# Local attention in units of 58 queries and 64 keys, both heads of a pair in one transpose

## The chip, the cores and the metric

One core of a Trainium2 chip runs the whole program. The metric is the device time of one execution in microseconds (us). PE (TensorE) does matrix products and transposes, DVE (VectorE), ACT (ScalarE) and POOL (GpSimd) work on elements, SP only issues DMAs.

## What is computed

Three stages in a row; the change touches the first alone. Here S = 576, D = 64, four sequences of eight heads.

```python
q_d, k_d, v_d = means over groups of 4 positions          # 144 groups
out_d = softmax(q_d @ k_d.T / 8) @ v_d                     # the "down" half
mask = abs(pos[:, None] - pos[None, :]) < 4                # 7 keys a query
out_local = softmax(where(mask, q @ k.T / 8, -1e9)) @ v    # the "local" half
x = repeat(out_d, 4) + out_local                           # 2304 tokens x 512
x = (silu(x @ w_gate) * (x @ w_val)) @ w_out               # 512 -> 1536 -> 512
# then each token goes to one of 8 experts: relu(x @ w1[e]) @ w2[e], times its gate
```

## The kernel before, in words

Heads are taken two at a time: 16 **pairs**, n = 0 to 15, four to a sequence b. A pair has five slots of 128 x 1024 floats: `sq` (queries, later also sums), `sk` (keys), `sv` (values for the local half), `sd` (values for the down half), `sa` (local scores). In `sq` and `sk` the first head has partitions 0 to 63, the second 64 to 127.

**Local half** (`local`, L569; `local_piece`, L610). Nine units of 64 queries with a window of 70 keys. L582 makes the scores of a unit, two units stacked to a block of 128 partitions x 70; L588 adds the mask, L591 to L601 take the softmax over 700 columns with L595 on ACT, and L603 on POOL divides. L628 transposes each block of each head by itself (70 x 128), in three pieces; ACT copies them out of PSUM at L632 and L636, the two large ones into `sd`, which first has to be free of the down half (`vfree`). L652 multiplies with the values, 70 rows deep, both heads of a pair into the two halves of one PSUM bank; L659 on DVE adds the down half and writes `x32`.

**Down half** (`down`, L491). L496 sums groups of four, L506 makes scores, L522 exponentials, L531 divides, L539 transposes, and L556 multiplies with v. For pairs 0 to 7 (`n < NE`) the sum of four values is left to L556 as sixteen products (profiles and traces count an fp32 product as two instructions, so 32 there); for pairs 8 to 15 POOL sums first (`down_v`, L486 and L488) and L556 has four products.

**Gated layer.** 9 chunks of 256 tokens; L750 is the first product (gate and val), L782 the second. The first two chunks go through the six weight blocks together, as the blocks come. A weight block is decoded from 64-bit words: L339 (DVE), L342 and L346 (ACT), L349 (DVE), L354 (ACT), L356 (POOL). Sequence 0 supplies chunk 0 and 1, sequence 1 is worked off beside these chunks' products, sequences 2 and 3 beside chunks 2 to 5. For pairs 4 to 7 the two heads' scores are made one after the other (`head_sets`).

**Order.** The program writes its instructions with a planner (`Sched`): every step is a task with a priority and a cost in ns, and the planner's simulated time decides the order in which the steps stand on each engine. At run time each engine takes its list strictly in that order. So any change of a cost or a dependency can move steps everywhere. While nothing is ready before the first chunk, `keep_warm` fills PE with products that nobody reads (L314). Pairs 4 to 7 reuse the slots of pairs 0 to 3, and their loads stand on SP among the weight loads (L330).

Of the kernel before, what the change touches and what calls it, by code (L numbers as in the profile page):

```python
# [19 lines left out]
ALU = mybir.AluOpType  # L20
# [12 lines left out]
NU = S // 64  # L33
WK = 70
NPAIR = (NU + 1) // 2
# [30 lines left out]
def t_act(n): return 170 + 0.85 * n  # L66
# [140 lines left out]
EARLY_N = range(NE)  # L207
WEIGHT_P = [1.0, 2.0, 3.0, 4.0, 4.5, 4.8]


def build(tc, a):
# [26 lines left out]
    def dma(n):  # L238
        return ("op", "DMA", t_dma(n), None)
# [197 lines left out]
    def heads(n):  # L437
        b, hp = divmod(n, HP)
        cls, tk = ("we", "early") if n in EARLY_N else ("aw", "late")
        if b > 1:  # L440

            for j in range(2):
                yield ("wait", ("w_out", NFB - 1, j))
        yield ("get", tk)
        sl = []
        for _ in range(5):
            sl.append((yield ("get", cls)))
        sq, sk, sv, sd, sa = sl
        src = a["qk"][b, hp]
        yield dma(P * 1158 * 4)  # L450
# [40 lines left out]
    def down(n, sq, sk, sd):  # L491

        qd = sq[:, S:S + 2 * G].rearrange("p (j g) -> p j g", j=2)
# [4 lines left out]
        st = sk[:GH, 710:726].rearrange("p (i x) -> p i x", i=4)  # L498
# [59 lines left out]
        if n < NE:  # L558
            sc.set(("vfree", n))
        yield op("ACT", t_act(G))  # L560
        nc.scalar.copy(sq[:, S + 2 * G:S + 3 * G], av[:, 0:G])
# [5 lines left out]
    def local(n, sq, sk, sv, sa, st):  # L567
# [3 lines left out]
        A = sa[:, 0:2 * m].rearrange("p (h c) -> p h c", h=2)  # L571
        A3 = sa[:, 0:2 * m].rearrange("p (x w) -> p x w", w=WK)
        mx, s1 = sa[:, 2 * m:2 * m + 2 * NPAIR], sa[:, 2 * m + 2 * NPAIR:2 * m + 4 * NPAIR]
        bc = lambda x: x.unsqueeze(2).to_broadcast([P, 2 * NPAIR, WK])
        for hs in head_sets(n):
            sp = yield from pget(len(hs))
            yield op("PE", 1000)
            for u in range(2 * NPAIR):
                uu = min(u, NU - 1)
                for h2, s in zip(hs, sp):  # L580
                    r = slice(h2 * D, (h2 + 1) * D)
                    nc.tensor.matmul(s[(u % 2) * 64:(u % 2) * 64 + 64, u // 2 * WK:(u // 2 + 1) * WK],  # L582
                                     sq[r, 64 * uu:64 * uu + 64], sk[r, 64 * uu:64 * uu + WK], start=True, stop=True)
            if hs[-1] == 1:
                sc.set(("qk", n))
            for h2, s in zip(hs, sp):
                yield op("DVE", t_dve(m) + 60)
                nc.vector.tensor_tensor(out=A[:, h2], in0=s[:, 0:m], in1=amask, op=ALU.add)  # L588
                pput(s)
# [14 lines left out]
        for jj in range(3):  # L604
            sc.spawn(sc.cur.prio, local_piece(n, jj, sq, sk, sv, sa, st, A))
# [3 lines left out]

    def local_piece(n, jj, sq, sk, sv, sa, st, A):  # L610

        b, hp = divmod(n, HP)
        vl = lambda u: sv[:WK, u * P:(u + 1) * P] if u < NU - 1 else sk[:WK, S + 6:S + 6 + P]
        js = [j for j in (2 * jj, 2 * jj + 1) if j < NPAIR]
        if jj < 2:
# [7 lines left out]
        yield op("PE", 2 * len(js) * 75)  # L623
# [5 lines left out]
        k = 2 * len(js) * P  # L629
        if jj == 2:  # L630
            yield op("ACT", t_act(P))
            nc.scalar.copy(t.rearrange("p (h q) -> p h q", h=2)[:, :, 0:64],  # L632
                           tp[:WK, 0:2 * P].rearrange("p (h q) -> p h q", h=2)[:, :, 0:64])
        else:
            yield op("ACT", t_act(k))
            nc.scalar.copy(t[:, 0:k], tp[:WK, 0:k])  # L636
        pput(tp)
        t0, t1 = 256 * jj, min(S, 256 * jj + 256)
# [5 lines left out]
        yield op("PE", 4 * len(js) * 65)  # L644
        for i, j in enumerate(js):
            for u in (2 * j, 2 * j + 1):
                if u >= NU:
                    continue
                for h2 in range(2):
                    o = (2 * i + h2) * P + u % 2 * 64  # L650
                    c = (u - 4 * jj) * 64
                    nc.tensor.matmul(xp[h2 * D:(h2 + 1) * D, c:c + 64], vl(u)[:, h2 * D:(h2 + 1) * D], t[:, o:o + 64],  # L652
                                     start=True, stop=True)
        up = sq[:, S + 2 * G:S + 3 * G]
        while t0 < t1:
# [5 lines left out]
                in0=xp[:, t0 - 256 * jj:e - 256 * jj].rearrange("p (g f) -> p g f", f=4),  # L661
# [666 lines left out]
def consts():  # L1328

    m = np.full((2, 64, NPAIR, WK), NEG, np.float32)  # L1330
    for u in range(2 * NPAIR):
        for q in range(64):
            for w in range(7):
                key = 64 * min(u, NU - 1) + q + w - 3
                if 0 <= key < S:
                    m[u % 2, q, u // 2, q + w] = 0.0
# [14 lines left out]
def layout(inputs):  # L1351
# [3 lines left out]
    qk = np.zeros((B, HP, 2, D, 2 * S + 6), q.dtype)  # L1355
    qk[..., 0:S] = q.transpose(0, 1, 2, 4, 3)
    qk[..., S + 3:2 * S + 3] = k.transpose(0, 1, 2, 4, 3)
    arr["qk"] = qk.reshape(B, HP, P, 2 * S + 6)

    vp = np.zeros((B, HP, S + 6, 2, D), v.dtype)  # L1360
    vp[:, :, 3:S + 3] = v.transpose(0, 1, 3, 2, 4)
    vv = np.zeros((B, HP, GH, NU * P + 1024), v.dtype)
    for u in range(NU):
        vv[:, :, 0:WK, u * P:(u + 1) * P] = vp[:, :, 64 * u:64 * u + WK].reshape(B, HP, WK, P)
    vv[..., NU * P:] = v.reshape(B, HP, 2, 2, GH, 4 * D).transpose(0, 1, 4, 2, 3, 5).reshape(B, HP, GH, 1024)
    arr["vv"] = vv
# [20 lines left out]
```

## Time and profile before

| | |
|---|---|
| median of 3 runs | 928.62 us (926.08 to 933.64) |
| the profiled execution, its own time | 932.92 us |
| its span, first to last instruction | 931.1 us |
| PE busy | 903.5 us (97%) |
| DVE, ACT, POOL busy | 438.5, 403.1, 279.5 us |

The profile's own time lies 4.3 us above the median of the runs. In its rows a line such as "L628 PE MATMUL" is line 628 of the kernel; two instructions of PE may overlap, so how long a group keeps PE is read from its start to the start of what follows.

### The profile page before, as it was taken

How to read it: one execution, taken by the hardware profiler on the slowest of the kernel's cores; microseconds unless marked ns; L12 is line 12 of the kernel's file. 1: busy time of each engine (PE TensorE's matmuls, PEld its weight loads, DVE VectorE, ACT ScalarE, POOL GpSimd, SP SyncE). 2: the span in 40 equal slices, each digit the busy share in tenths (PEclk: the TensorE clock that was granted, in tenths of full speed). 3: DMA queues.
4: the chain of work that ended last, by engine and by line, in shares of the span. 5: the costliest groups of instructions: out<-in, count | busy, mean ns of one | idle time of the engine just before them, and what ended most of it. 6: DMA issues, size and time to landing. Idle time of an engine off the chain costs nothing. (4 is left out here: it accounts for less than half of the span.)

```text
span 931.1 us, 17520 instructions
## 1 busy us (share of the span) xinstructions
PE 903.5 (97%) x7039; PEld 797.3 (86%) x7046; DVE 438.5 (47%) x1020; ACT 403.1 (43%) x867; POOL 279.5 (30%) x286
## 2 busy tenths in 40 slices
PE   8999899999999999999999999999999999999995
PEld 4688788998999989889999999989888888888883
DVE  4949756744435435454323231456544554544310
ACT  1678679954235224333332231345334444444221
POOL 1335535633324323324212121231220412321211
PEclk9969999999999999999999999999999999999997
DMA  8745334411211212022000000146256544554100
GB/s 211 211 156 167 104 125 136 128 58 50 76 38 40 54 53 70 8 53 76 2 22 3 1 25 1 49 155 204 58 172 201 182 153 162 174 179 134 35 25 27
DMA packets 52869, 87.90 MB, mean 94 GB/s; under 512 B 7982, under 2 KB 25614, under 8 KB 52784
## 3 DMA queue, kind: packets, MB, share of 16 engines
q1 hardware_dynamic: 48048, 76.59, 27.1%
q0 software_dynamic: 4160, 9.48, 3.0%
q8 instruction: 56, 0.92, 0.4%
q10 hardware_dynamic: 576, 0.67, 0.3%
q14 instruction: 29, 0.24, 0.1%
HBM read 77.73 MB, written 10.57 MB: 95 GB/s over the span
## 5 line engine op out<-in xcount | busy, mean ns | idle before, releaser
L750 PE MATMUL ps<-xhi,w 128*128 128x256 f32 x1536 | 304.7, 288 | 2.9 <-ACT aw L522 1.4
L750 PEld LDWEIGHTS ps<-xhi,w 128*128 128x128 f32 x1536 | 247.9, 191 | 10.2 <-issue 3.5
L750 PE MATMUL ps<-xlo,w 128*128 128x256 f32 x768 | 217.6, 283 | 0.3 <-POOL xlo L707 0.3
L750 PEld LDWEIGHTS ps<-xlo,w 128*128 128x128 f32 x768 | 147.3, 192 | 2.0 <-POOL xlo L707 0.5
L720 DVE SCALAR_TENSOR_TENSOR th<-th,ps 128x256 f32<-128x256 f32 x108 | 45.3, 419 | 183.6 <-ACT th L718 183.5
L1076 PE MATMUL ps<-xh,w 128*128 128x336 f32 (+1 forms) x512 | 121.9, 313 | 0.0
L782 PE MATMUL x<-w,hh 128*128 128x512 f32 x384 | 121.2, 397 | 0.4 <-ACT hh L725 0.4
L728 POOL TENSOR_TENSOR hl<-th,hh 128x256 fp32r<-128x256 f32 x90 | 69.7, 774 | 166.3 <-ACT hh L725 136.1
L718 ACT ACTIVATE th<-ps 128x256 f32<-128x256 f32 x108 | 41.7, 386 | 157.9 <-PE ps L750 152.1
L1076 PEld LDWEIGHTS ps<-xh,w 128*128 128x128 f32 x512 | 87.9, 188 | 2.1
L975 DVE TENSOR_TENSOR w<-w,w 128x1024 fp32r<-128x1024 f32 x64 | 77.5, 1224 | 16.2 <-ACT w L973 14.7
L1086 PE MATMUL x<-w,eh 128*128 128x512 f32 x256 | 81.0, 397 | 0.0
L1076 PE MATMUL ps<-xl,w 128*128 128x336 f32 (+1 forms) x256 | 79.8, 312 | 0.0
L782 PEld LDWEIGHTS x<-w,hh 128*128 128x128 f32 x384 | 68.2, 188 | 13.0 <-ACT hh L725 0.8
L1062 DVE SCALAR_TENSOR_TENSOR el<-ps,eh 128x336 fp32r<-128x336 f32 (+1 forms) x64 | 31.5, 492 | 101.0 <-ACT eh L1060 97.8
L1101 POOL DMA_INDIRECT out<-t,tb x23 | 22.9, 994 | 180.1 <-ACT t L1093 165.0
L1060 ACT ACTIVATE eh<-ps 128x336 fp32r<-128x336 f32 (+1 forms) x64 | 28.4, 443 | 108.7 <-PE ps L1076 107.5
L782 PE MATMUL x<-w,hl 128*128 128x512 f32 x192 | 75.0, 390 | 0.2 <-DVE hl L728 0.2
L725 ACT CAST hh<-th 128x256 fp32r<-128x256 f32 x108 | 44.2, 409 | 61.0 <-DVE th L722 60.8
L973 ACT CAST w<-w 128x1024 fp32r<-128x1024 f32 x64 | 66.0, 1044 | 0.0
L1086 PEld LDWEIGHTS x<-w,eh 128*128 128x128 f32 x256 | 46.5, 188 | 9.2
L356 POOL TENSOR_TENSOR w<-w,w 128x512 fp32r<-128x512 f32 x30 | 40.4, 1352 | 36.0 <-ACT w L354 17.4
(195 smaller groups left out, 1464.5 us busy)
## 6 DMA issues: line engine op xcount, KB each, us to landing
w<-w SPq DMA_DIRECT2D x64, 512.0 KB
w<-w_gate SPq DMA_DIRECT2D x10, 512.0 KB
w<-w_val SPq DMA_DIRECT2D x10, 512.0 KB
w<-w_out SPq DMA_DIRECT2D x10, 512.0 KB
x2d<-t SPq DMA_DIRECT2D x18, 256.0 KB
w<-qk SPq DMA_DIRECT2D x8, 291.0 KB
aw<-qk SPq DMA_DIRECT2D x8, 291.0 KB
w<-qk SPq DMA_DIRECT2D x8, 288.0 KB
```

What stands on the lines that cost most here:

```text
L356: nc.gpsimd.tensor_tensor(out=los, in0=lw.bitcast(F32), in1=his, op=ALU.subtract)
L718: nc.scalar.activation(th, ps[:, 0:CT], AF.Tanh, scale=0.5)
L720: nc.vector.scalar_tensor_tensor(out=th, in0=th, scalar=1.0, in1=ps[:, 0:CT], op0=ALU.add, op1=ALU.mult)
L725: nc.scalar.copy(hh[:, j].bitcast(F32R), th)
L728: e.tensor_tensor(out=hl[:, j].bitcast(F32R), in0=th, in1=hh[:, j].bitcast(F32R), op=ALU.subtract)
L750: nc.tensor.matmul(ps[:, o:o + CT], ww[:, k, fs], xx[:, k, :], start=(k == 0 and n == 0), stop=(k == KD - 1 and n == 2))
L782: nc.tensor.matmul(x2p[c, m], l[:, j, ms], r[:, js], start=(p == 0 and j == 0 and n == 0), stop=(p == NFB - 1 and j == 1 and n == 2))
L973: nc.scalar.copy(hi.bitcast(F32R), raw)
L975: nc.vector.tensor_tensor(out=lo.bitcast(F32R), in0=raw, in1=hi.bitcast(F32R), op=ALU.subtract)
L1062: nc.vector.scalar_tensor_tensor(out=hl[:, j, 0:n].bitcast(F32R), in0=ps[:, 0:n], scalar=0.0, in1=hh[:, j, 0:n].bitcast(F32R), op0=ALU.max ...
L1076: nc.tensor.matmul(ps[:, 0:n], ww[:, k, fs], xx[:, k, 0:n], start=(k == 0 and t == 0), stop=(k == KD - 1 and t == 2))
L1086: nc.tensor.matmul(yt[:m], l, r, start=(first and n == 0), stop=(last and n == 2))
```

## The change

Ten units of 58 queries and 64 keys replace nine of 64 and 70. A block of 128 partitions now holds 64 columns of one head and 64 of the other, so one full 128 x 128 transpose does both heads; after it the first head's keys stand on partitions 0 to 63 and the second's on 64 to 127. The values come in that layout as a new input `vw`. The transposed pieces go into free parts of `sv` and `sa` and no longer wait for `vfree`. The sums of v go to POOL for pairs 4 to 7 as well (`NV = 4` in place of `NE = 8`). The pieces end at 232, 464 and 576 queries (256, 512 and 576 before). The scores compute 64 query rows per unit of which 58 are used.

```diff
-NU = S // 64
-WK = 70
-NPAIR = (NU + 1) // 2
+UQ = 58
+NU = -(-S // UQ)
+WK = UQ + 6
+NPAIR = NU // 2
+SP6 = S + 6
+unit0 = lambda u: min(UQ * u, S - UQ)
...
+NV = 4
@@ heads @@
-        nc.sync.dma_start(out=sq[:, 0:S], in_=src[:, 0:S])
-        nc.sync.dma_start(out=sk[:, 0:S + 6], in_=src[:, S:2 * S + 6])
+        nc.sync.dma_start(out=sq[:, 0:SP6], in_=src[:, 0:SP6])
+        nc.sync.dma_start(out=sk[:, 0:SP6], in_=src[:, SP6:2 * SP6])
         sc.cur.t -= sc.LAT_DMA
-        vs = a["vv"][b, hp]
-        yield dma(GH * 2176 * 4)
-        nc.sync.dma_start(out=sv[:WK, :], in_=vs[:WK, 0:1024])
-        nc.sync.dma_start(out=sk[:WK, S + 6:S + 6 + P], in_=vs[:WK, 1024:1152])
-        nc.sync.dma_start(out=sd[:GH, :], in_=vs[:, 1152:2176])
+        yield dma(P * NU * D * 4 + GH * 4096)
+        nc.sync.dma_start(out=sv[:, 0:NU * D], in_=a["vw"][b, hp])
+        nc.sync.dma_start(out=sd[:GH, :], in_=a["vv"][b, hp])
         pr = sc.cur.prio
-        if n >= NE:
+        if n >= NV:
             sc.spawn(pr, down_v(n, sk, sd))
@@ down (the same in both places where n < NE stood) @@
-        if n < NE:
+        if n < NV:
             parts = [sd[:GH, 256 * x + D * i:256 * x + D * (i + 1)] for x in range(4) for i in range(4)]
@@ local @@
-        A = sa[:, 0:2 * m].rearrange("p (h c) -> p h c", h=2)
+        A = sa[:, 0:2 * m].rearrange("p (j h w) -> p j h w", h=2, w=WK)
...
-            for u in range(2 * NPAIR):
-                uu = min(u, NU - 1)
+            for u in range(NU):
+                t0 = unit0(u)
                 for h2, s in zip(hs, sp):
                     r = slice(h2 * D, (h2 + 1) * D)
                     nc.tensor.matmul(s[(u % 2) * 64:(u % 2) * 64 + 64, u // 2 * WK:(u // 2 + 1) * WK],
-                                     sq[r, 64 * uu:64 * uu + 64], sk[r, 64 * uu:64 * uu + WK], start=True, stop=True)
+                                     sq[r, t0:t0 + 64], sk[r, t0:t0 + WK], start=True, stop=True)
...
@@ local_piece @@
-            t = st[:WK, jj * 512:(jj + 1) * 512]
-            yield ("wait", ("vfree", n))
-        else:
-            t = sa[:WK, 740:996]
+        k = len(js) * P
+        t = (sv[:, 640:896], sa[:, 680:936], sv[:, 896:1024])[jj]
         [tp] = yield from pget()
...
         for i, j in enumerate(js):
-            w = min(P, S - j * P)
-            for h2 in range(2):
-                o = (2 * i + h2) * P
-                nc.tensor.transpose(tp[:WK, o:o + w], A[:w, h2, j * WK:(j + 1) * WK], ident[:w, :w])
...
+            nc.tensor.transpose(tp[:, i * P:(i + 1) * P], sa[:, j * P:(j + 1) * P], ident)
+        yield op("ACT", t_act(k))
+        nc.scalar.copy(t, tp[:, 0:k])
         pput(tp)
-        t0, t1 = 256 * jj, min(S, 256 * jj + 256)
+        t0, t1 = 4 * UQ * jj, min(S, 4 * UQ * (jj + 1))
+        p0 = t0
...
-                    nc.tensor.matmul(xp[h2 * D:(h2 + 1) * D, c:c + 64], vl(u)[:, h2 * D:(h2 + 1) * D], t[:, o:o + 64],
-                                     start=True, stop=True)
+                    r = slice(h2 * D, (h2 + 1) * D)
+                    nc.tensor.matmul(xp[r, UQ * u - p0:UQ * u - p0 + UQ - o], sv[r, u * D:(u + 1) * D],
+                                     t[r, i * P + v * 64 + o:i * P + v * 64 + UQ], start=True, stop=True)
```

On PE, in the products of chunk 3, pair 9 of sequence 2 is transposed and multiplied with its values (`ps` is a PSUM bank, `aw` a slot of the pair, `cn` holds the identity; xN counts like rows in a row). Transposes before, and now:

```order
1465 L750 MATMUL ps_1_104<-xhi,w_4_1861 128x256
1466 L628 MATMUL ps_1_103<-cn,aw_3_2730 70x128 x4
1467 L628 MATMUL ps_1_102<-cn,aw_3_2730 70x128 x4
1468 L628 MATMUL ps_1_107<-cn,aw_3_2730 70x64 x2
1469 L750 MATMUL ps_1_106<-xhi,w_5_1698 128x256
```

```order
1471 L740 MATMUL ps_1_102<-xhi,w_3_1774 128x256
1472 L624 MATMUL ps_1_107<-cn,aw_3_2662 128x128 x2
1473 L624 MATMUL ps_1_106<-cn,aw_3_2662 128x128 x2
1474 L624 MATMUL ps_1_103<-cn,aw_3_2662 128x128
1475 L740 MATMUL ps_1_102<-xhi,w_3_1772 128x256
```

Products with v of the same pair, before, and now:

```order
1507 L782 MATMUL x_1_108<-w_3_1687,hl_1_97 128x512
1508 L652 MATMUL ps_1_104<-aw_3_2729,aw_4_2728 64x64 x8
1509 L652 MATMUL ps_1_107<-aw_3_2729,aw_4_2728 64x64 x8
1510 L652 MATMUL ps_1_105<-aw_3_2730,aw_4_2727 64x64 x2
1511 L750 MATMUL ps_1_103<-xhi,w_3_1938 128x256
```

```order
1519 L740 MATMUL ps_1_107<-xhi,w_5_1854 128x256
1520 L642 MATMUL ps_1_103<-aw_4_2660 64x58 x8
1521 L642 MATMUL ps_1_102<-aw_3_2662,aw_4_2660 64x58 x8
1522 L642 MATMUL ps_1_105<-aw_4_2660 64x58 x2
1523 L642 MATMUL ps_1_105<-aw_4_2660 64x54 x2
1524 L740 MATMUL ps_1_107<-xhi,w_6_1853 128x256
```

Ten transposes become five; eighteen products become twenty, and both heads of a piece still go into one bank. The places among the large products are nearly the same.

On SP, where the loads of pairs 5 and 6 meet the second weight block (gate, gate, val, val), before, and now:

```order
34 L451 DMA w_2_645<-qk 128x576
35 L452 DMA w_2_646<-qk 128x582
36 L456 DMA w_2_647<-vv 70x1024
37 L457 DMA w_2_646<-vv 70x128
38 L458 DMA w_2_648<-vv 72x1024
39 L330 DMA w_1_643<-w_gate 128x2x512
40 L330 DMA w_2_702<-w_gate 128x2x512
41 L330 DMA w_2_717<-w_val 128x2x512
42 L451 DMA w_2_797<-qk 128x576
43 L452 DMA w_2_798<-qk 128x582
```

```order
28 L460 DMA w_2_532<-vv 72x1024
29 L334 DMA w_2_505<-w_gate 128x2x512
30 L334 DMA w_2_599<-w_val 128x2x512
31 L455 DMA w_2_650<-qk 128x582
32 L456 DMA w_2_651<-qk 128x582
33 L459 DMA w_2_652<-vw 128x640
34 L460 DMA w_2_653<-vv 72x1024
35 L334 DMA w_2_619<-w_val 128x2x512
36 L455 DMA w_2_766<-qk 128x582
37 L456 DMA w_2_767<-qk 128x582
```

Before, the block's second val load stood behind the loads of pairs 6 and 7; now it stands ahead of both.

On POOL, from the decode of the first weight block on, before, and now (`hl`, `xlo` belong to the gated layer, 72x4x128 and 72x256 are the sums of v):

```order
23 L356 TENSOR_TENSOR w_1_146<-w_1_141,w_1_145 128x512
24 L356 TENSOR_TENSOR w_1_146<-w_1_142,w_1_145 128x512
25 L356 TENSOR_TENSOR w_1_369<-w_1_346,w_1_368 128x512
26 L393 TENSOR_TENSOR ess<-ess,half 8x1
27 L356 TENSOR_TENSOR w_1_369<-w_1_367,w_1_368 128x512
```

```order
19 L360 TENSOR_TENSOR w_1_146<-w_1_141,w_1_145 128x512
20 L360 TENSOR_TENSOR w_1_146<-w_1_142,w_1_145 128x512
21 L697 TENSOR_TENSOR xlo<-x_1_112,xhi 128x256
22 L697 TENSOR_TENSOR aw_1_117<-x_1_113,aw_1_116 128x256
23 L488 TENSOR_TENSOR w_2_532<-w_2_532 72x4x128
24 L360 TENSOR_TENSOR w_1_369<-w_1_346,w_1_368 128x512
25 L490 TENSOR_TENSOR w_2_530<-w_2_532 72x256
26 L606 TENSOR_TENSOR w_1_137<-w_1_137 128x640
```

The sums of pair 4 (w_2_530, w_2_532) now stand ahead of the division of pair 3 (w_1_137), which before stood ahead of the whole decode.

## Rows read from the trace of the kernel before

**Rows 1.** Page: span; busy time, share of the span and instructions of PE and its loads.

```profile
span 931.1 us, 17520 instructions
PE 903.5 (97%) x7039; PEld 797.3 (86%) x7046; DVE 438.5 (47%) x1020; ACT 403.1 (43%) x867; POOL 279.5 (30%) x286
```

**Rows 2.** Stretches: length, busy (instructions) by engine, granted clock, DMA share, GB/s.

```profile
51.10:68.20 17.10, 17.10 (x129) 14.96 (x129) 5.53 (x10) 11.07 (x18) 5.90 (x6) 0.50 0.51 165
68.20:112.60 44.40, 41.20 (x437) 35.56 (x437) 38.79 (x81) 34.58 (x76) 26.13 (x23) 1.00 0.41 120
112.60:119.40 6.80, 6.80 (x32) 5.80 (x30) 1.52 (x6) 2.27 (x8) 2.53 (x3) 0.50 0.68 269
119.40:205.00 85.60, 84.68 (x745) 76.04 (x744) 53.71 (x105) 70.62 (x122) 44.89 (x39) 1.00 0.37 118
205.00:480.00 275.00, 272.67 (x2495) 247.85 (x2494) 123.28 (x385) 96.88 (x281) 87.42 (x100) 1.00 0.16 44
```

**Rows 3.** Groups by line: busy us, mean ns of one, idle before and its releasers.

```profile
L314 PE MATMUL x<-w 128*128 128x512 bf16 x113 | 29.0, 404 | 2.9 <-POOL w L311 2.1 <-issue 0.6 <-DMA w<-vv 0.2
```

**Rows 4.** Order of time on PE, sequences 2 and 3: start us, us, instruction.

```profile
287.12 0.66 PE L827 MATMUL x<-cn,t 128*128 128x128 f32 x4
287.53 0.36 PE L750 MATMUL ps<-xhi,w 128*128 128x256 f32 x1
...
300.19 0.71 PE L556 MATMUL ps<-aw 72*64 72x144 f32 x8
...
302.45 1.27 PE L652 MATMUL ps<-aw,aw 70*64 70x64 f32 x36
303.65 0.39 PE L750 MATMUL ps<-xhi,w 128*128 128x256 f32 x1
...
313.77 0.84 PE L582 MATMUL ps<-aw,aw 64*64 64x70 f32 x40
...
324.68 1.27 PE L628 MATMUL ps<-cn,aw 128*70 128x128 f32 x10
325.88 0.72 PE L782 MATMUL x<-w,hh 128*128 128x512 f32 x2
```

**Rows 5.** Order of time on PE, sequence 1.

```profile
121.51 0.83 PE L582 MATMUL ps<-w,w 64*64 64x70 f32 x20
...
134.11 2.18 PE L556 MATMUL ps<-w,w 72*64 72x144 f32 x32
```

**Rows 6.** Waits of PE, 0 to 215 us: total, times, longest.

```profile
PE ps L750 <- POOL w L356: 1.2, 1, 1.2
```

**Rows 7.** Order of time: a block's last decode on POOL, its first use on PE.

```profile
151.53 1.32 POOL L356 TENSOR_TENSOR w<-w,w 128x512 fp32r<-128x512 f32 x1
158.95 0.39 PE L750 MATMUL ps<-xhi,w 128*128 128x256 f32 x1
187.30 1.31 POOL L356 TENSOR_TENSOR w<-aw,w 128x512 fp32r<-128x512 f32 x1 [0.20 <-ACT w L354]
196.51 0.40 PE L750 MATMUL ps<-xhi,w 128*128 128x256 f32 x2
```

**Rows 8.** Groups by line on ACT and POOL, columns as in rows 3.

```profile
L636 ACT COPY aw<-ps 70x512 f32<-70x512 f32 x16 | 8.7, 582 | 4.0 <-PE ps L628 3.3 <-POOL aw L531 0.6
L542 ACT COPY aw<-ps 72x288 f32<-72x288 f32 x16 | 6.3, 392 | 8.1 <-PE ps L539 7.8
L486 POOL TENSOR_TENSOR aw<-aw 72x512 f32<-72x512 f32 x8 | 10.3, 1288 | 8.3 <-DMA aw<-vv 8.3
L488 POOL TENSOR_TENSOR aw<-aw 72x256 f32<-72x256 f32 x8 | 5.9, 733 | 0.5
```

**Rows 9.** Order of time on ACT and SP: in brackets the idle time before and its releaser.

```profile
62.88 0.28 ACT L561 COPY w<-ps 128x144 f32<-128x144 f32 x1 [2.91 <-PE ps L556]
66.60 0.35 SPq L451 DMA_DIRECT2D w<-qk  x1
75.24 0.40 SPq L330 DMA_DIRECT2D w<-w_val  x1
```

More of the change, by code (lines that the diff above doesn't have):

```diff
@@ L557, in down @@
                                      start=(kh == 0 and i == 0), stop=(kh == 1 and i == k - 1))
-        if n < NE:
+        if n < NV:
             sc.set(("vfree", n))
         yield op("ACT", t_act(G))
-        nc.scalar.copy(sq[:, S + 2 * G:S + 3 * G], av[:, 0:G])
+        nc.scalar.copy(sq[:, SP6 + 2 * G:SP6 + 3 * G], av[:, 0:G])
         pput(av)
@@ L587, in local @@
                 yield op("DVE", t_dve(m) + 60)
-                nc.vector.tensor_tensor(out=A[:, h2], in0=s[:, 0:m], in1=amask, op=ALU.add)
+                nc.vector.tensor_tensor(out=A[:, :, h2, :], in0=s[:, 0:m].rearrange("p (j w) -> p j w", w=WK),
+                                        in1=amask.rearrange("p (j w) -> p j w", w=WK), op=ALU.add)
                 pput(s)
@@ L608, in local, with local_piece @@
         sc.set(("done", n))
-    def local_piece(n, jj, sq, sk, sv, sa, st, A):
+    def local_piece(n, jj, sq, sv, sa):
         b, hp = divmod(n, HP)
-        vl = lambda u: sv[:WK, u * P:(u + 1) * P] if u < NU - 1 else sk[:WK, S + 6:S + 6 + P]
         js = [j for j in (2 * jj, 2 * jj + 1) if j < NPAIR]
-        if jj < 2:
-            t = st[:WK, jj * 512:(jj + 1) * 512]
-            yield ("wait", ("vfree", n))
-        else:
-            t = sa[:WK, 740:996]
+        k = len(js) * P
+        t = (sv[:, 640:896], sa[:, 680:936], sv[:, 896:1024])[jj]
         [tp] = yield from pget()
         yield ("lag", SLACK)
-        yield op("PE", 2 * len(js) * 75)
+        yield op("PE", len(js) * 107)
         for i, j in enumerate(js):
-            w = min(P, S - j * P)
-            for h2 in range(2):
-                o = (2 * i + h2) * P
-                nc.tensor.transpose(tp[:WK, o:o + w], A[:w, h2, j * WK:(j + 1) * WK], ident[:w, :w])
[L629 to L636, printed above, removed]
+            nc.tensor.transpose(tp[:, i * P:(i + 1) * P], sa[:, j * P:(j + 1) * P], ident)
+        yield op("ACT", t_act(k))
+        nc.scalar.copy(t, tp[:, 0:k])
         pput(tp)
-        t0, t1 = 256 * jj, min(S, 256 * jj + 256)
+        t0, t1 = 4 * UQ * jj, min(S, 4 * UQ * (jj + 1))
+        p0 = t0
         yield ("wait", ("up", n))
@@ L643, in local_piece @@
         yield ("lag", SLACK)
-        yield op("PE", 4 * len(js) * 65)
+        yield op("PE", 4 * len(js) * 60)
         for i, j in enumerate(js):
-            for u in (2 * j, 2 * j + 1):
-                if u >= NU:
-                    continue
+            for v in range(2):
+                u = 2 * j + v
+                o = UQ * u - unit0(u)
                 for h2 in range(2):
-                    o = (2 * i + h2) * P + u % 2 * 64
-                    c = (u - 4 * jj) * 64
-                    nc.tensor.matmul(xp[h2 * D:(h2 + 1) * D, c:c + 64], vl(u)[:, h2 * D:(h2 + 1) * D], t[:, o:o + 64],
-                                     start=True, stop=True)
-        up = sq[:, S + 2 * G:S + 3 * G]
+                    r = slice(h2 * D, (h2 + 1) * D)
+                    nc.tensor.matmul(xp[r, UQ * u - p0:UQ * u - p0 + UQ - o], sv[r, u * D:(u + 1) * D],
+                                     t[r, i * P + v * 64 + o:i * P + v * 64 + UQ], start=True, stop=True)
+        up = sq[:, SP6 + 2 * G:SP6 + 3 * G]
         while t0 < t1:
@@ L1330, in consts @@
     m = np.full((2, 64, NPAIR, WK), NEG, np.float32)
-    for u in range(2 * NPAIR):
+    for u in range(NU):
         for q in range(64):
-            for w in range(7):
-                key = 64 * min(u, NU - 1) + q + w - 3
-                if 0 <= key < S:
+            for w in range(min(7, WK - q)):
+                if 0 <= unit0(u) + q + w - 3 < S or q >= UQ:
                     m[u % 2, q, u // 2, q + w] = 0.0
@@ L1353, in layout @@
     q, k, v = (inputs[x].reshape(B, HP, 2, S, D) for x in "qkv")
-    qk = np.zeros((B, HP, 2, D, 2 * S + 6), q.dtype)
+    qk = np.zeros((B, HP, 2, D, 2 * SP6), q.dtype)
     qk[..., 0:S] = q.transpose(0, 1, 2, 4, 3)
[L1357 to L1366, printed above, removed]
+    qk[..., SP6 + 3:SP6 + 3 + S] = k.transpose(0, 1, 2, 4, 3)
+    arr["qk"] = qk.reshape(B, HP, P, 2 * SP6)
+    vp = np.zeros((B, HP, 2, SP6, D), v.dtype)
+    vp[..., 3:S + 3, :] = v
+    vw = np.stack([vp[..., unit0(u):unit0(u) + WK, :] for u in range(NU)], axis=4)
+    arr["vw"] = np.ascontiguousarray(vw).reshape(B, HP, P, NU * D)
+    arr["vv"] = np.ascontiguousarray(v.reshape(B, HP, 2, 2, GH, 4 * D).transpose(0, 1, 4, 2, 3, 5)).reshape(B, HP, GH, 1024)
     arr["w_gate"] = words(inputs["moe_w_gate"])
```

16 lines of the change are left out of this document (8 added, 8 removed).

## The prediction

> **What bounds the kernel.** I read the page first, then the stretches, the waits of PE, the groups by line and last the order of time. The page has PE busy for 903.5 of 931.1 us and no other engine over half [rows 1]. So PE's work is the time, unless PE is busy with nothing or at half speed. The stretches show where that is. From 205 to 480 us, where sequences 2 and 3 run beside the gated layer, PE is busy 272.67 of 275 us at a granted clock of 1.00: an instruction saved there is time saved. From 119.4 to 205 us it is 84.68 of 85.6, but ACT is at 70.62 and hands out weight blocks just ahead of PE. From 51.1 to 68.2 and from 112.6 to 119.4 us the granted clock is 0.50, the 1.2 GHz level, with PE busy all the time [rows 2]; in the first of these ACT waits for PE (2.91 us at one copy alone [rows 9]), so PE is the bound there too, at half speed. At the very start PE is not the bound: 113 products that nobody reads fill 29.0 us there [rows 3].
>
> **PE's work in pairs 8 to 15.** Durations are taken at full clock, from one start to the next [rows 4].
> - Transposes: ten from 324.68 to 325.88, 1.20 us. The new form, 128 x 128 with a full stationary side, is in the trace at L827: four in 287.12 to 287.53, 0.1025 us each, so five take 0.51. Gain 0.69; at the old pace of 0.12 each it would be 0.60.
> - Scores: 40 instructions in 0.84 us, with 70 columns. With 64 the gain is at most 0.07, at least nothing; I take 0.05.
> - Products with v: 36 instructions from 302.45 to 303.65, 1.20 us or 33 ns each. Each uses all the rows of the array for one head and half the columns, and two heads' products overlap. The new ones use half the rows and half the columns, a different half of both for each head. No row shows that form. Upper gain: the scores, which use four such quarters, pass one in 0.84 / 40 = 21 ns, so 40 would take 0.84, a gain of 0.36. Lower end: the two heads' products don't overlap; 2 x 33 x 58/64 = 60 ns, 40 take 2.42, a loss of 1.22. The nearest row is L652 itself, two products at a time into one bank: 33 x 58/64 = 30 ns, 40 take 1.21. I take no change.
>
> Sum for a pair: 0.69 + 0.05 = 0.74; eight pairs 5.9 us. No wait covers it in that stretch.
>
> **Pairs 4 to 7.** The same transposes, 0.69. The scores are made head by head here, and 20 instructions take 0.83 us where 40 take 0.84, so the fewer columns give up to twice as much, 0.10. The products of the down half fall from 32 instructions (2.18 us [rows 5]) to 8 (0.71 [rows 4]), 1.47. Together 2.26 a pair, 9.0 us for four. POOL takes over their sums: 1288 + 733 ns a pair [rows 8], 8.1 us in all, where it is busy 44.89 of 85.6 us and 26.13 of 44.4 [rows 2]. I cost this at nothing. Queued behind the first of these sums are the last two decodes of the first weight block and pair 3's division; the sum waits for pair 4's values to land, and if they were late, pair 3 would wait with them.
>
> **Pairs 0 to 3.** 4 x 0.74 = 3.0 us, but ahead of the first products PE has the fillers of [rows 3] to give up instead. The part that falls into the half-clock stretch would count double, up to 6 us; the lower end is nothing.
>
> **What the weights allow.** In the fourth of the six blocks the last gate or val decode ends at 151.53 + 1.32 = 152.85 us and PE first uses it at 158.95, 6.1 us later; in the sixth 188.61 and 196.5, 7.9 us [rows 7]. PE can come earlier by that much and no more, plus what ACT gains: the two large copies of a pair go from 512 to 256 columns, 582 to about 392 ns (the 288-column copy [rows 8]), 0.38 us a pair, 3.0 us for the eight pairs before 205 us. So some 9 to 11 us. The second block already made PE wait 1.2 us [rows 6]. There two things move against each other. Its second val load stood behind pair 6's load, which was issued at 66.60, and went out at 75.24 [rows 9]; now it stands ahead. But the attention of sequence 1 is pulled ahead of this block on DVE, ACT and POOL, and DVE has just 44.4 - 38.79 = 5.6 us free there [rows 2]. I take these two as even; the ends are a gain of 1.2 and a loss of 5.
>
> So of 9.0 us for pairs 4 to 7 and 0 to 6 for the head I let 8.5 through to the end of these chunks. The rest is at no cost: the loads of a pair are four instead of five and 1.22 MB in place of 1.21 by their shapes, with the DMA engines busy 0.16 to 0.41 of the time outside the head and the half-clock stretches [rows 2]; 640 in place of 700 columns on DVE and POOL shortens their work; the new ends of the pieces give pairs 0 to 3 two more small additions each on DVE, about what these columns save.
>
> **Sum.** 8.5 + 5.9 = 14.4 us. The profiled execution's own time is 932.92 us (931.1 of span and 1.8 around it), so 918.5 on its own scale. That run lies 4.3 above the median of 928.62; against the median it is 914.2. I predict 914.
>
> **A rule that speaks against the change.** In the rows, products into one bank share the same rows of the array (L652), and products on different rows (L582 in these pairs) go to two banks, one a head. The new products with v put both heads, on different rows, into one bank, and no row shows how they run. The Trainium skill's page "TensorEngine Tiling (Array Packing)", section "Restrictions and Gotchas", says that different row tiles cannot access the same PSUM bank at the same time. No run here shows it so far. By that rule each product would wait for the other head's, and the time would be that of the first rival below; by the row of L652 it would not, and the sum stands.
>
> **Rivals.**
> - *The heads take turns.* If the products with v don't overlap, each pair loses 1.22 us of the array and 16 pairs 19.5, against a gain of 14.4. That gives 928.6 + 5.1 = 934, slower. It decides the sign from the point where a product takes 52 ns: the gain of 14.4 us over 16 x 40 products is 22 ns each, on top of the 30 taken above. For it: the two heads had a bank each in the scores. Against: the two heads' results go to different partitions of the bank, and L652 already has two heads writing to the two halves of one bank at 33 ns. Chance 0.13.
> - *The weights take it.* The attention of sequence 1 ahead of the second block holds up the decode, or the half-clock stretch grows because the small products now stand closer together; what pairs 0 to 7 save comes back as waits of PE for L356 or as slow products. Then the late pairs' 5.9 us alone remain: 922.7. For it: ACT at 83% and a slack of 6 to 8 us. Against: ACT's own work falls too, and the blocked load is freed. Chance 0.23.
> - *The head gains more.* The 17.1 us at half clock cost 8.5 us, and PE was the bound in them. The pieces no longer wait for the down half, and sequence 0 has less work. If that stretch goes or shrinks, up to 8.5 us more: 906. Against: what went before it, PE busy with small attention steps and fillers, is still there. Chance 0.14.
>
> **How the numbers follow.** The forecast has 0.50 and its own range is 909.5 to 919.5 (a gain of 9 to 19: the bounds of transposes and scores, and 0 to 6 us of the head). With the second and third rival it holds 0.87; I cut at 906 and 926, which leaves out the first rival and the edges, 0.2. One per cent, 9.3 us, is about what a measurement of this kernel tells from no change. Faster than 919.3: the forecast (0.48), the third rival (0.14) and a little of the second, 0.64. Within 1%: most of the second, and half of the first, 0.30. Slower: 0.06.
>
> **What would show it.** Right: transposes at about 0.10 us each, 40 products with v in 1.2 us, eight instructions of the down half's product in pairs 4 to 7, and PE as full as before from 200 us on. The first use of the last block's second val half, 196.5 us before [rows 7], comes at about 188; from there to the end the new kernel gains another 5 to 6 us. Wrong: 40 products with v in 2.4 us (first rival); new waits of L740 for L360 of several us between 85 and 200, or more time at 0.50 (second); much less than 17.1 + 6.8 us at a granted clock of 0.50 (third).

## The result, and the profile after

The changed kernel takes 916.39 us (median; 915.09 to 917.9) against 927.47 us of the kernel before, run beside it (926.08 to 933.64): a ratio of 0.9868, 95% interval 0.9819 to 0.9918. 914 was predicted, with a range of 906 to 926. The executions of the kernel before lie in two groups: of the 63 beside the experiments 37 took 922.2 to 927.0 us and 26 took 930.4 to 935.6. The profile ahead of the prediction (932.92) is of the upper group. A second profile of it, taken below, is of the lower (925.94). The ten executions of the changed kernel (four here, six at the end of the experiments) lie between 914.7 and 918.2.

The page of the changed kernel, span and engines, to set beside [rows 1]:

```profile
span 913.3 us, 17270 instructions
PE 886.4 (97%) x6928; PEld 785.4 (86%) x6934; DVE 443.7 (49%) x1028; ACT 395.4 (43%) x867; POOL 287.9 (32%) x294
```

PE is still busy for 97% of the span: 17.1 us less work, 17.8 us less span. Its stretches, columns and bounds as in [rows 2]:

```profile
40.00:51.10 11.10, 8.93 (x165) 7.04 (x162) 8.67 (x25) 10.45 (x27) 3.70 (x3) 0.99 0.74 214
51.10:68.20 17.10, 14.54 (x151) 12.95 (x153) 13.63 (x26) 9.61 (x27) 11.51 (x11) 0.60 0.59 179
68.20:112.60 44.40, 44.04 (x430) 38.19 (x427) 35.18 (x81) 34.09 (x83) 29.52 (x27) 0.89 0.33 108
112.60:119.40 6.80, 6.80 (x75) 5.77 (x75) 4.59 (x10) 6.17 (x9) 3.86 (x3) 1.00 0.81 249
119.40:205.00 85.60, 85.56 (x670) 78.31 (x669) 56.33 (x107) 65.33 (x119) 45.95 (x41) 1.00 0.36 118
205.00:480.00 275.00, 272.88 (x2544) 250.60 (x2543) 124.53 (x404) 95.41 (x286) 89.49 (x104) 1.00 0.14 42
```

The half clock has moved, not gone. The granted clock is 0.50 from 50.9 to 61.1 and from 64.5 to 78.2 us, 23.9 us together; in the profile of before the two stretches of [rows 2] are 23.9 us as well. ACT from 119.4 to 205 us has fallen from 70.62 to 65.33, POOL has risen by 1 us only.

Order of time on PE in the late pairs, to set beside [rows 4] (start us, us, instruction; L642 are the products with v, L584 the scores, L624 the transposes):

```profile
227.13 0.68 PE L642 MATMUL ps<-aw 64*64 64x58 f32 x16
227.64 0.63 PE L642 MATMUL ps<-aw,aw 64*64 64x58 f32 x16
228.21 0.38 PE L740 MATMUL ps<-xhi,w 128*128 128x256 f32 x1
...
229.90 0.44 PE L642 MATMUL ps<-aw 64*64 64x58 f32 x8
230.27 0.38 PE L740 MATMUL ps<-xhi,w 128*128 128x256 f32 x1
...
239.78 0.81 PE L584 MATMUL ps<-aw,aw 64*64 64x64 f32 x40
240.52 0.39 PE L740 MATMUL ps<-xhi,w 128*128 128x256 f32 x1
...
251.39 0.71 PE L624 MATMUL ps<-cn,aw 128*128 128x128 f32 x5
251.85 0.36 PE L740 MATMUL ps<-xhi,w 128*128 128x256 f32 x1
...
259.81 0.68 PE L642 MATMUL ps<-aw 64*64 64x58 f32 x16
260.32 0.63 PE L642 MATMUL ps<-aw,aw 64*64 64x58 f32 x16
260.79 0.40 PE L642 MATMUL ps<-aw 64*64 64x58 f32 x8
261.12 0.38 PE L740 MATMUL ps<-xhi,w 128*128 128x256 f32 x1
```

Five full transposes take 0.46 us, 92 ns each, where ten took 1.20. The 40 scores take 0.74 from their start to the start of what follows. Read in the same way they took 0.78 before; the 0.84 of [rows 4] is the group's own length, which runs on beside the products of the next line:

```profile
313.77 0.84 PE L582 MATMUL ps<-aw,aw 64*64 64x70 f32 x40
314.55 0.73 PE L782 MATMUL x<-w,hh 128*128 128x512 f32 x2
```

The products with v are 40 now. In six of the eight late pairs they stand in one group and take 1.31 us (259.81 to 261.12), where 36 took 1.20. In the other two pairs they are given in two groups: 1.08 us from 227.13 to 228.21 and 0.37 from 229.90 to 230.27, so 1.45. Within a group 16 take 0.51, 32 ns each.

The last block's second val half, to set beside the last two rows of [rows 7]: on POOL its last decode, on PE its first use.

```profile
179.16 1.32 POOL L360 TENSOR_TENSOR w<-aw,w 128x512 fp32r<-128x512 f32 x1 [2.63 <-ACT w L358]
...
184.30 0.40 PE L740 MATMUL ps<-xhi,w 128*128 128x256 f32 x2
```

It is used at 184.4 us, the second product of that row, 12.1 us earlier than before; it was ready at 180.5, 8.1 us earlier. So PE took 4 of the 7.9 us that lay between them, and the decode itself came earlier by more than the 3.0 us that ACT was said to gain. The same decode and first use in the second profile of the kernel before:

```profile
181.12 1.31 POOL L356 TENSOR_TENSOR w<-aw,w 128x512 fp32r<-128x512 f32 x1 [0.17 <-ACT w L354]
...
190.40 0.40 PE L750 MATMUL ps<-xhi,w 128*128 128x256 f32 x2
```

There the decode is ready at 182.4 us, 6.2 us earlier than in the first profile of the same program, and PE comes 6.1 us earlier.

PE's longest waits of the first 215 us, to set beside [rows 6] (total, times, longest):

```profile
PE x L318 <- POOL w L315: 2.1, 1, 2.1
PE ps L740 <- ACT aw L524: 1.2, 1, 1.2
```

The wait for a decode (L356 before, L360 now) is gone; the first row is the fillers' own start, the second is at 213.8 us.

Where the time came from is read by setting the same product of the two traces side by side and taking the difference of their starts. By how much the changed kernel is ahead, in us, at a place named by its own time:

```
                                     165    274    465    590    end
of the profile shown before         12.2   12.3   18.0   18.0   17.8
of the second profile of before      6.1    6.2   11.9   11.9   10.8
```

Pairs 8 to 15 run from 206 to 446 us. From 165 to 465 us both columns give the same, 5.8, so 0.72 us a pair. (Up to 274 us almost nothing of it is seen: by then the changed kernel has given pair 10's first scores as well, and it waits 0.56 us longer behind pair 8's transposes.) Ahead of 165 us the columns differ by 6.1. That is most of the 7.0 us between the two profiles of before, and in the second the end agrees with the medians (927.47 - 916.39 = 11.1).

### The profile page after: what moved, and what is told of

The parts are those of the page before. It is cut to its first block, busy times and chain, and to the rows that moved or that the text cites. A ratio compares the mean times of both kernels' runs of the same rounds, so it can differ in the third digit from the quotient of the medians.

```text
span 913.3 us, 17270 instructions
## 1 busy us (share of the span) xinstructions
PE 886.4 (97%) x6928; PEld 785.4 (86%) x6934; DVE 443.7 (49%) x1028; ACT 395.4 (43%) x867; POOL 287.9 (32%) x294
## 5 line engine op out<-in xcount | busy, mean ns | idle before, releaser
L360 POOL TENSOR_TENSOR w<-w,w 128x512 fp32r<-128x512 f32 x30 | 41.2, 1382 | 29.4 <-ACT w L358 24.6
```

The source lines that it names most:

```text
L360: nc.gpsimd.tensor_tensor(out=los, in0=lw.bitcast(F32), in1=his, op=ALU.subtract)
```

## The experiments

**The kernel before, once more**

> The kernel before, nothing changed, for a second profile: its times lie in two groups, 922 to 926 and 931 to 936, and the profile shown is one of the upper. If the upper group's extra lies in the stretches at a granted clock of 0.50, a profile of the lower group has less than the 23.9 us of them before 205 us, and the rest of its order of time is the same to 1 us.

925.94 us, span 924.1. Its stretches, columns as in [rows 2]:

```profile
51.10:68.20 17.10, 15.78 (x231) 13.63 (x229) 11.84 (x23) 14.16 (x28) 9.61 (x10) 1.00 0.85 248
...
84.00:112.60 28.60, 25.72 (x224) 21.73 (x222) 20.52 (x47) 19.33 (x46) 15.05 (x13) 0.89 0.32 108
112.60:119.40 6.80, 6.80 (x76) 5.58 (x74) 3.56 (x6) 5.44 (x10) 2.19 (x2) 0.96 0.00 0
```

The same program with the same instructions has 1.00 where [rows 2] has 0.50, from 51.1 to 68.2 us. Only 6.8 us at 0.50 are left (106.3 to 113.1). It gains 6.1 us on the first profile between 51 and 68 us, and keeps them. Half of 17.1 us would be 8.5; 1.0 of the difference are waits of PE that the second profile has and the first has not, and the other 1.4 show that the half clock cost less than half of its length here. The mean granted clock is on record for every execution: it is 0.986 to 0.994 in all 37 of the lower group and 0.975 to 0.982 in all 26 of the upper. So the clock, not the program, tells the two groups of executions apart; that it is this stretch is seen in one profile of each.

**Sums of v on TensorE for sequence 1 as well**

```diff
-NV = 4
+NV = 8
```

> The changed kernel, but pairs 4 to 7 leave the sums of v to TensorE again (32 instructions of the down half's product a pair in place of 8). Theory A, the time saved is the PE work saved: 4 x 1.47 = 5.9 us come back, 916.4 + 5.9 = 922. Rival B, in the first two chunks the weight blocks set the pace and PE's savings there were waits anyway: 916 to 918.

921.27 us (919.52 to 925.26), ratio 0.9934 (0.9901 to 0.9966): 4.9 us slower than the change. In the chunk's products a row of pairs 4 to 7 reads as in [rows 5] again:

```profile
127.44 2.18 PE L558 MATMUL ps<-w,w 72*64 72x144 f32 x32
129.55 0.71 PE L508 MATMUL ps<-w 64*72 64x144 f32 x4
```

The 24 products more are 1.47 us a pair, 5.9 for four, and 4.9 is seen between the medians. The median of the mean granted clock is nearly the same in both (0.976 to 0.977), so these 4.9 us are not the clock's. The profile alone would not show it: it is of a slower execution (923.77) and lies 9.4 us behind the change from 148 us on, but with 34.1 us at half clock before 205 us where the change has 23.9, so some 5 of the 9.4 are the clock's. In this order POOL does these sums at little cost.

**The same sums moved to POOL, in the kernel before**

```diff
+NV = 4
...
-        if n >= NE:
+        if n >= NV:
             sc.spawn(pr, down_v(n, sk, sd))
...
-        if n < NE:
+        if n < NV:
```

> The kernel before with one part of the change alone: POOL sums v for pairs 4 to 7. Theory A: 927.5 - 5.9 = 921.6. Rival B: no gain, 926 to 928, since weight blocks or POOL's 8 us of new work take it.

926.92 us (923.59 to 935.88), ratio 1.0 (0.996 to 1.0039): nothing. Its stretches:

```profile
51.10:68.20 17.10, 14.92 (x209) 12.94 (x209) 11.68 (x18) 13.25 (x25) 13.76 (x13) 0.82 0.75 235
68.20:84.00 15.80, 15.80 (x124) 14.62 (x122) 11.65 (x24) 10.31 (x20) 7.66 (x8) 0.87 0.57 178
84.00:112.60 28.60, 25.02 (x208) 21.41 (x206) 24.33 (x47) 19.14 (x41) 18.13 (x15) 0.88 0.13 37
112.60:119.40 6.80, 6.67 (x52) 5.81 (x52) 3.30 (x11) 5.10 (x14) 3.78 (x4) 1.00 0.79 246
119.40:205.00 85.60, 83.25 (x698) 74.18 (x697) 55.99 (x112) 71.60 (x129) 47.24 (x40) 1.00 0.37 124
```

Against the second profile of before it is 1.3 us behind at 171 us, though PE has 5.9 us less to do. It is at half clock from 62.2 to 72.4 and from 92.9 to 99.7 us, 17.0 us in place of 6.8: 5.1 us. And from 84 to 205 us PE is busy 25.02 + 6.67 + 83.25 = 114.9 us where it was 117.2: 2.3 us more of waiting. 5.1 + 2.3 - 5.9 = 1.5. This is the second rival as it was described, in another kernel: what the edit saves comes back as half clock and as waits. It is worth 5 us in the new order and nothing in the old one.

**Sums of v on POOL for every pair**

```diff
-NV = 4
+NV = 0
```

> The changed kernel with the sums of the values on POOL for every pair, sequence 0 too. Array time: 24 products of about 0.06 us fewer in each of four pairs, 1.47 us a pair, 5.9 us in all; POOL gets 2.0 us a pair more, 8.1 us. Theory of the first use (what PE saves ahead of the first gate products is taken by fillers, and the loads of the weights set that time): 915 to 918, no change. Theory array: what is saved comes through at least in part, 910 to 914. Theory POOL: the sums stand in the way of the first decodes, PE waits for them: 918 to 922.

910.6 us (909.5 to 911.92), ratio 0.9817 (0.9773 to 0.9862); the change beside it on the same chip 916.03 (914.68 to 918.2). Its stretches, and PE around its longest wait:

```profile
40.00:51.10 11.10, 6.82 (x82) 5.69 (x83) 9.13 (x27) 10.09 (x31) 8.18 (x7) 0.70 0.74 223
51.10:78.30 27.20, 26.73 (x276) 22.83 (x275) 21.89 (x47) 18.48 (x44) 19.57 (x18) 0.62 0.60 192
78.30:112.60 34.30, 30.78 (x301) 25.96 (x300) 26.02 (x59) 27.52 (x59) 20.41 (x18) 0.95 0.34 112
```

```profile
94.23 0.38 PE L624 MATMUL ps<-cn,w 128*128 128x128 f32 x2
98.14 0.41 PE L407 MATMUL ps<-cn,t 8*128 8x8 f32 x4 [3.52 <-DVE t L403]
98.48 0.39 PE L740 MATMUL ps<-xhi,w 128*128 128x256 f32 x1
```

The fastest kernel of this study, and the number that array time gave, but by luck. Its trace does not show 5.9 us in the head: it is 2.0 us ahead of the changed kernel from 148 us on. PE has some 9 us less to do there (an estimate, busy time at half clock counted half; nine fillers fewer are a part of it), but 30.7 us at half clock before 205 us (23.9 in the change) and more waits, a new one of 3.52 us at L407 among them. So what PE no longer does is mostly spent again there. The next 2.5 us come in one step near 600 us, where nothing was edited (last section). The medians with eight, four and no pairs on TensorE, 921.27, 916.03 and 910.6, are 5.2 and 5.4 us apart, but the second step is not array time alone.

**The products with v head by head**

```diff
-        for i, j in enumerate(js):
-            for v in range(2):
-                u = 2 * j + v
...
-                for h2 in range(2):
-                    r = slice(h2 * D, (h2 + 1) * D)
+        for h2 in range(2):
+            r = slice(h2 * D, (h2 + 1) * D)
+            for i, j in enumerate(js):
+                for v in range(2):
...
```

> The changed kernel with the products with v of a piece given head by head, so that two that follow each other use the same half of the array. Nothing else moves. If the gain hangs on the two heads' products overlapping in one bank: each goes from about 32 to about 60 ns, 40 x 28 = 1.1 us a pair, 13 us for pairs 4 to 15 and up to 18 with the head, 929 to 934. If they do not overlap already, or overlap whatever their order: 916 to 918, with 31 to 34 ns each as now.

922.89 us (919.65 to 925.99), ratio 0.9941 (0.9905 to 0.9976): 6.5 us slower than the change. PE, the first 32 products of a pair:

```profile
231.96 0.78 PE L642 MATMUL ps<-aw 64*64 64x58 f32 x13
232.52 0.26 PE L642 MATMUL ps<-aw,aw 64*64 64x58 f32 x1
...
232.74 0.73 PE L642 MATMUL ps<-aw,aw 64*64 64x58 f32 x13
233.41 0.39 PE L740 MATMUL ps<-xhi,w 128*128 128x256 f32 x1
```

They take 1.45 us where the heads in turn take 1.08, so giving them in turn is worth 0.37 us for these 32. The 45 ns of one are an average. The trace has the start of every product; here are those of the first piece, in ns from the group's first, with the same from the kernel before (head by head the two are told apart by their pace):

```
before, both heads           0, 7  107, 113  165, 172  223, 230  282, 288  340, 347  398, 405  457, 463
heads in turn, both heads    0, 6  102, 108  160, 167  218, 224  277, 283  335, 341  393, 400  452, 458
head by head, first head     0  102  160  218  277  335  393  452
head by head, second head    282  384  442  501  559  617  676  734
```

After the first, a head's products follow each other at 58 ns, whatever the order, and also in the kernel before, with 64 columns. With the heads in turn the two heads' products start 6 ns apart in one bank; head by head, the second head starts when half of the first head's are given, so half of each run still has a partner. A product without a partner costs 58 ns, near the 60 of the prediction's lower end. The loss is less than half of what was expected because this order takes the partner from only half of the products. In pairs 8 to 15 the trace falls back by 3.3 us, 0.41 a pair. Ahead of them it is 4.9 us behind, with 30.7 us at half clock where the change has 23.9, so some 3.4 of the 4.9 are the clock's.

**Each transpose twice**

```diff
-            nc.tensor.transpose(tp[:, i * P:(i + 1) * P], sa[:, j * P:(j + 1) * P], ident)
+            for _ in range(2):
+                nc.tensor.transpose(tp[:, i * P:(i + 1) * P], sa[:, j * P:(j + 1) * P], ident)
```

> The changed kernel with each full transpose given twice into the same place; the order of all other steps stays. Five more a pair at the 0.092 us that the profile after shows: 0.46 us a pair. Theory A: 12 pairs that nothing covers 5.5 us, all sixteen 7.4, so 922 to 924. Rival B: what pairs 0 to 7 add is covered by waits for weights, 8 x 0.46 = 3.7 us alone, 920.

917.59 us (916.56 to 919.77), ratio 0.9894 (0.9844 to 0.9944); its executions overlap with the change's. Ten transposes of a late pair on PE:

```profile
252.27 1.25 PE L625 MATMUL ps<-cn,aw 128*128 128x128 f32 x10
253.28 0.36 PE L741 MATMUL ps<-xhi,w 128*128 128x256 f32 x1
```

1.01 us. In pairs 8 to 15 the kernel falls back 3.8 us, 0.47 a pair, as five more at 92 ns give. In pairs 0 to 7, with the same eight times five, it loses 0.9 us in all. The end is only 1.9 us later, since 2.8 us are gained near 600 us. So an instruction of the late pairs is paid in full, and one of the early pairs is paid a quarter. By the trace the early 3.7 us are all there as work of PE; against them stand 1.7 us less waiting and 3.4 us less at half clock (20.5 where the change has 23.9, some 1.1 of time).

**The order of before's costs**

```diff
-            yield op("PE", 920)
+            yield op("PE", 1000)
...
-        yield op("PE", len(js) * 107)
+        yield op("PE", len(js) * 150)
...
-        yield op("PE", 4 * len(js) * 60)
+        yield op("PE", 4 * len(js) * 65)
```

> The changed kernel with the planner's costs of scores, transposes and products with v set as they were before (1000, 75 a transpose of 70, 65): the same work in another order. Theory A, the work saved is the gain: 914 to 919. Rival C, the early part's gain is luck of one order: over 4 us away from 916, either side.

921.76 us (919.13 to 923.97), ratio 0.9919 (0.9886 to 0.9952): 5.4 us slower than the change with the same instructions, but for four fillers fewer. By its trace it is 6.5 us behind already at 98 us and 6.7 at 465. Two of its stretches:

```profile
51.10:68.20 17.10, 14.33 (x151) 11.88 (x153) 14.73 (x30) 8.48 (x24) 11.16 (x11) 0.63 0.54 179
68.20:84.00 15.80, 15.80 (x156) 13.64 (x153) 11.28 (x25) 9.49 (x26) 8.48 (x8) 0.54 0.46 138
```

Half clock lasts 30.8 us before 98 us here, 6.9 more than in the change, so 3.4 of the 6.5 us; PE's waits of over 0.3 us between 40 and 98 us sum to 6.5 us where the change has 4.6, 1.9 more. The other 1.2 are spread. So the early gain belongs to the order as much as to the work.

**The pieces wait for the down half again**

```diff
+        if jj < 2:
+            yield ("wait", ("vfree", n))
```

> The changed kernel, but the first two pieces of a pair wait for the down half's product with v again, as before the change. Theory D: taking this wait away is what brings sequence 1 and the decode of the weight blocks forward; with it the slack between decode and use goes back to about zero in blocks two and three and 3 to 6 us are lost: 919 to 922. Rival: only the work counts, 915 to 918.

919.2 us (916.32 to 921.6), ratio 0.9923 (0.9892 to 0.9954): 2.8 us slower by the medians, with executions that overlap. Its profile is 3.1 us behind from 148 to 600 us. The stretch:

```profile
51.10:68.20 17.10, 17.10 (x173) 15.22 (x175) 12.56 (x20) 11.70 (x25) 12.12 (x11) 0.50 0.60 191
68.20:84.00 15.80, 15.39 (x140) 12.95 (x136) 10.43 (x28) 8.19 (x24) 7.93 (x7) 0.57 0.54 172
```

34.1 us are at half clock (47.8 to 81.9), 10.2 more; half of that, 5.1, is more than the loss. The number came as expected, the reason did not: the last val decodes of the second and third block are ready 5.0 and 5.7 us before PE uses them, and PE waits for no decode, so it is not the weights that were made late.

**More fillers: until the third pair, and until all of sequence 0 is done**

```diff
-        while ("x", 0, 0) not in sc.ev:
+        while ("x", 0, 2) not in sc.ev:
```

```diff
-        while ("x", 0, 0) not in sc.ev:
+        while ("x", 0, HP - 1) not in sc.ev:
```

> The changed kernel, with the fillers of PE kept up until the last instead of the first pair's part of the first chunk is ready: 169 instead of 119, the 50 new ones among the small products of 40 to 78 us, where the profile after shows 23.9 us at a granted clock of 0.50, 12 us lost. If PE is given the full clock by being busy with large products, up to 12 us come back and the fillers, 50 x 0.22 = 11 us, cost what does not fit into PE's waits there (some 5 us): 908 to 915. Rival: the clock stays low, or the fillers only delay: 917 to 927.

> The changed kernel with fillers until the third attention pair of sequence 0 is done instead of the first: 145 fillers, between 119 and 169. Theory clock: fillers take array time (about 0.25 us each at full clock) and give back what the half clock costs; 26 of them cost up to 6.5 us where PE has no idle time, and save up to half of 23.9 us. If the half-clock stretch starts only once the fillers end, it is shortened but not gone: 914 to 917. If the early fillers are enough: 911 to 914, under the version with 169. Theory that the fillers only fill idle time and the clock has no part: 916, no change.

By the programs the changed kernel has 119 fillers, as the kernel before has (the 113 of [rows 3] are those that its trace holds), and with the first diff it has 145, with the second 169. 169: 913.54 us (909.7 to 914.58), ratio 0.9838 (0.978 to 0.9896). 145: 913.63 us (911.76 to 914.03), ratio 0.9848 (0.9803 to 0.9893). Of the first:

```profile
51.10:68.20 17.10, 15.04 (x184) 10.32 (x182) 14.17 (x27) 9.30 (x26) 11.51 (x10) 0.90 0.70 206
68.20:84.00 15.80, 15.80 (x192) 12.51 (x192) 14.61 (x33) 9.56 (x29) 10.56 (x10) 1.00 0.34 113
```

Half clock before 205 us is down to 3.4 us with 169 and 17.0 with 145, from 23.9. Yet both are 0.3 us behind the change from 148 to 590 us: the fillers cost what the clock and shorter waits give back. In the 145 the step near 600 us gives 2.8, in the profile of the 169 it does not; their medians are 2.4 to 2.9 us under the change, and where that comes from in the 169 is not shown.

**The kernel before with more fillers**

The last diff in the kernel before: by the programs 145 fillers in place of 119, of which the trace holds 135.

> The kernel before with fillers until all of sequence 0's attention is done: 139 instead of 113. Theory clock: the kernel before with its stretch at 0.50 from 51 to 68 us takes 931 to 935, without it 922 to 927; with more fillers the stretch goes in every execution, so the times above 930 vanish and the median stays at 922 to 927, since fillers cost about what they save. If the two groups have another cause: times above 930 as often as in the kernel before.

926.02 us (923.91 to 928.42), ratio 0.9994 (0.9965 to 1.0023). None of 12 executions is above 930, where 5 of 17 of the kernel before beside it were. The stretch:

```profile
51.10:68.20 17.10, 17.05 (x265) 13.67 (x264) 13.05 (x27) 14.94 (x33) 11.11 (x10) 1.00 0.78 236
```

So the upper group does hang on that stretch: with fillers in it, the clock is at 1.00 there in the profile, and 10.2 us at half clock come later (98.2 to 108.4 us).

**The changed kernel, once more**

> The changed kernel as it is, a second time, beside the variants with more fillers. If its time is set by its order alone: 915 to 918 again, and a profile with about 24 us at a granted clock of 0.50 before 205 us. If the granted clock differs from one execution to the next, as it did between two profiles of the kernel before (23.9 us and 6.8 us), the sum at 0.50 should differ here too, by 10 us or more, and the end of the first two chunks' products (202.6 us) by some 0.5 us for each us of it.

916.03 us (914.68 to 918.2), ratio 0.9882 (0.9837 to 0.9927). Half clock from 50.9 to 61.2 and from 64.6 to 78.3 us, 24.0 together; its products stand within 0.2 us of the first profile's up to 612 us. In the changed kernel the half clock came twice in the same place; in the kernel before it came in one profile and not in the other. But both profiles of the change are of executions with a mean granted clock of 0.980, the highest of its ten. The other eight have 0.975 to 0.978, which is 4 to 9 us more at half clock (twice the difference, of 914 us) that no profile shows.

## Why the prediction was right

**Pairs 8 to 15: right in size; the transposes are right in mechanism too.** 5.9 us were predicted, 5.8 measured. All starts of PE between the same two large products (204.0 and 468.6 us of the changed kernel), in both traces, give the terms for the eight pairs:

- Transposes: 5.5 us predicted, 5.5 gained.
- Scores: 0.4 predicted, 0.2 gained. The sum took the group's length, 0.84, where from start to start it was 0.77 to 0.78.
- Products with v: nothing predicted, 0.8 lost. This term failed. It scaled 33 ns by the columns, 58 of 64, to 30. But in [rows 4]'s group the products of one half of the array followed each other at 58 ns with 64 columns, and now they do so at 58 ns with 58. So four more are two rounds more, 0.1 us a pair, and more where they are given in two groups.

That is 4.9 us. The other 0.9 has no term in the sum: 0.2 less waiting, and 0.7 at products that the change does not touch, 0.3 of it at the second product of the gated layer. That they make the sum come out is luck.

**The first rival (heads take turns) is out.** Two heads' products start 6 ns apart in one bank, and the pace of each head is 58 ns with the other head beside it or not. The Trainium skill's page "TensorEngine Tiling (Array Packing)", section "Restrictions and Gotchas", says that different row tiles cannot access the same PSUM bank at the same time. As the prediction took it, that each product would wait for the other head's, this is not so in these runs. Whether the two write to the bank at the same moment is not shown.

**Pairs 0 to 7: the amount let through was mis-sized.** 8.5 us were predicted. Against the profile on which the sum was made it is 12.2; both profiles have 23.9 us at half clock, and 12.0 us of array time were reckoned, so no part of it was kept back. The failed term is "what the weights allow", 9 to 11 us. It took the decodes to come earlier only by ACT's own saving, 3.0 us; they came 8.1 earlier. In the second profile of before ACT has the same work as in the first, and the decode still comes 6.2 us earlier, together with PE. So the decodes move with PE's own work; how much they lay ahead of it bounded no gain here. Through which wait they follow was not traced.

Against the second profile of before, which is what the median stands for, it is 6.1 us, 2.4 less than predicted. Here the changed kernel pays 23.9 us at half clock against 6.8. By the traces up to the product at 204.0 us, with PE's busy time at half clock counted half (an estimate; between the two profiles of before it comes out 1.4 us too high): 12.8 us less work and 1.1 less waiting, and 7.8 more for the clock, which leaves 6.1. The clock's share is what the second rival names. The prediction took the half clock of the shown profile for a fixed property of the kernel before. It was one execution's.

**So the sum of 14.4 was right between two readings**: 17.8 against its own profile, 10.8 to 11.1 against the usual execution. That 914 lay only 2.4 us under the median is in part luck: the sum was 3.3 us too large for the usual execution, and the 928.62 that it was taken off lay 1.2 us above the median that the result gives.

**The sums on POOL at no cost** held for pairs 4 to 7 to within 1 us (4.9 of 5.9 us seen between the medians), but only in the new order. In the old order the same edit gave nothing.

**The third rival (the half clock goes)** did not happen. Against the usual execution of the kernel before, the half clock grew; when fillers did remove it, the fillers cost as much.

What stays open: what decides whether the clock falls in the head, since PE was busy 8.93 of 11.1 us ahead of the fall in the changed kernel and 9.78 and 9.95 in the two profiles of before, of which one fell; and why the wait and the half clock near 600 us differ between orders.

## What to carry to other kernels

Cost a saving where the bounding engine is full and at full clock, and set the rows of the edited steps side by side afterwards: the sum for the late pairs came out to 0.1 us with one term off by 0.8. Count small products by rounds, what one part of the array takes one after the other, and not by their columns. Where the clock is halved in the head, take two profiles before you reckon with it, and compare the mean clock of all executions: one execution's half clock was worth 6 us here. An edit that frees the bound engine early can be worth everything or nothing by the order that goes with it, so time it within the new order. When a move of work to an idle engine pays in part of the pairs, try the rest: putting the sums of pairs 0 to 3 on POOL too gave another 5.4 us, though not all of it for the reason expected.

## What the runs showed of the hardware

- Small products on one part of the array start every 58 ns at full clock, with 58 or 64 columns (61 ns with 70); those on other parts start 6 to 7 ns later beside them. So a product costs 58 ns alone, 29 with two parts in turn and 15 with four, and a group some 0.15 us more for its edges: 1.31 us for 40 on two quarters, 0.74 for 40 scores on four. The two quarters' results lay in one bank.
- The clock was granted at 1.00 or 0.50 for the same instructions in the same place of one program, in different executions. Ahead of the 0.50, PE ran small attention products with short waits in between. Fillers of 128 x 512 among them kept it at 1.00 from 51 to 68 us in the kernel before. In the changed one, fillers up to 58.7 or 77.8 us put the fall off from 50.9 to some 62 us.
- Near 604 us the changed kernel has a wait of 2.35 us at the transposes of L1025, for which the profile shows no releaser, and then 3.4 us at 0.50. At the same transposes the kernel before waits 2.0 and 2.4 us in its two profiles, for the DMA of their input, with the clock at 1.00. Five variants of the changed kernel pass this place 1.8 to 2.8 us quicker, with a wait of 0.9 to 2.1 us, and have the 0.50 between 655 and 673 us instead, where they lose 0.8 to 1.8 us again. Shifts of that size at a place that no edit touches are a part of every difference above that is under 3 us.
